# A gated linear recurrence with a solve in front: its lead-in in another order, products and zeroing on other engines

## The chip, the cores and the metric

The kernel runs on one core of a Trainium2 chip. Time is device time of one launch, in microseconds (us), as the median of three runs. Engines: PE is TensorE, DVE is VectorE, ACT is ScalarE, POOL is GpSimd, SP is SyncE, which issues most DMAs. A "q" behind an engine (SPq) is its queue.

## The reference, cut to what matters

```python
# attention part: B, H, S, D = 4, 8, 768, 40
for t in range(S):
    y[:, :, t] = np.einsum('bhd,bhde->bhe', rt, state)
    Sa = np.einsum('bhde,bhe->bhd', state, at)
    state_decay = state * wt[:, :, None, :] - np.einsum('bhd,bhe->bhde', Sa, bt)
    state = state_decay + np.einsum('bhd,bhe->bhde', vt, kt)
# then, on the 3072 rows of y: a mixture of 8 experts (top 2 by noisy logits),
# then w_in, h * tanh(softplus(h)), w_out
```

## The kernel before, in words

The 32 heads' sequences of 768 steps are cut into 24 chunks of C = 32 steps. A chunk is taken in two halves of 16 heads, so the state passes through NG = 48 turns of the recurrence; turn g belongs to chunk g // 2. Inside a chunk the steps are made independent by a triangular system, and chunks are solved four at a time (GJ = 4): solve 0 serves chunks 0 to 3 (turns 0 to 7), solve 1 chunks 4 to 7, and so on.

**Per chunk i.** `load_w` and `load` fetch w and a (tile wa), and k and b (tile kb). `scale` (L218) runs a decay scan E (L225), a reciprocal (L228), a backward scan R (L229) and the product abd (L234) on VectorE, then scales kb by R (L237, GpSimd); ScalarE makes copies (WE). `decays` (L244) copies E for the transposes. `prods` (L264) multiplies kb and abd on TensorE (L277) into a buffer of PSUM ring pp (two buffers); ScalarE copies it out twice (L282), to Ls, which goes to a DRAM scratch lscr, and to AM; `mask` (L285, GpSimd) masks the AM part. `turns` (L289) transposes kb and Ec on TensorE (L295) through ring pp; ScalarE copies the results to kn, which goes to DRAM and comes back into tile KB, and to EN. `scale_a` (L256) multiplies EN with AT (L261, a pair of GpSimd products) and asks for the AT load of chunk i + 2.

**Per four chunks.** `load_l` (L385) brings lscr back as tile Lu. `solve_group` (L388) inverts the triangular blocks in VectorE steps (L414, L416, then pairs of product L426 and reduction L429); solves 1 and on give two products to GpSimd. The result goes to DRAM (tscr, L463) and comes back in blocks (`tbd`, L357). `apply` (L364) multiplies blocks and AM on TensorE (L378) to tile Z.

**A turn of the recurrence** (`chain`, L586): s_mm (L541) and its VectorE eviction (L546, "s"), two groups of transposes `tr` (L558), u_mm of the next turn (L528), evicted by ScalarE (L531, "u eviction"), y_mm (L503), and rv_mm (L573) with its VectorE eviction (L584, "rv").

**The order** is written out by hand for TensorE, VectorE, ScalarE and GpSimd: what is emitted first runs first on its engine; SyncE issues in order of emission too. `begin` (L627) emits the lead-in of chunks 0 to 3. Then three generators (prepare, solve, apply) yield positions, and `pump` (L676) always advances the one with the lowest, up to the current one; a generator in `wants` can force another to go first. Positions of the lead-in are early(x) = -1 + x/42 (L315); turn c of the first eight stands at -.35 + 1.35 c/8 (`tau`, L622). Everything up to -.35 is emitted ahead of turn 0. Within a turn `pump` is called at (3, 6, 7, 8, 9, 9)/9 of it, the last two around rv_mm. Solve 0 advances x by the cost that its steps name:

```python
for t in range(1, h):                 # h = 8
    yield at(.38 + .0083 * t * t)
...
                yield at(.6)          # eight times
...
        yield at(.1 if i in pool else 1.2)   # pool is empty in solve 0
...
        yield at(1.2)                 # reductions, the last is add(5)
```

The OPT entry x places scale 4 at 4.6, the steps of chunk 4 at 5.2, of chunk 5 at 6.5, of chunk 6 at 12.5 and 21.5, of chunk 7 at 28; apply 0 stands at z0 = 20.9, and solve 1 at s_1, from -.45 to .6; because its load stands at -.51 and wants the products of chunks 4 to 7, these and scale 8 are emitted right behind solve 0.

Of the kernel before, what the change touches and what calls it, by code (L numbers as in the profile page):

```python
# [21 lines left out]
C = 32  # L22
# [5 lines left out]
OPT = dict(yd=(), yv=33, gix=(1, 3, 4), ye=(2, 2),  lag2=1, x=(4.6, 5.2, 6.5, 12.5, 21.5, 28, 28, 28), dl=0, dk=0, ns=(0, 0), nw=(1, 1), va=1, rb=0, ra=1, kb=0, ry=(2, 2), p1=(0, 0, 0, 1, 1, 1), lw=((4, 2, 2), (6, 6, 6)), fl=((0, 1, 2, 2, 2, 2, 2, 2), (0,) * 8), lag=6, ll=.06, hurry=40, pool=(1, 4), rvpool=False, f=(3, 3, 1, 1, 1, 0), s=(.05, .72), s_1=(-.45, .6), tl=1.9, zl=.96, zd=.32, t0=-.35, nd=3, z0=20.9)  # L28
# [37 lines left out]
class Rec:  # L66


    def __init__(self, ctx, nc, tc, ins, emit_x, ident, share, late):
# [15 lines left out]
        self.Y = {}  # L85
# [3 lines left out]
    def consts_a(self):  # L89
# [22 lines left out]
        self.d1b = []  # L112
        for i in range(2):
            t = one.tile([128, 2 * PR * (C + 1) + 1], F32, name=f"d1b{i}")
            nc.vector.memset(t, 0.0)
            self.d1b.append(t)
            self.abd.append(one.tile([128, PR, 2, C], F32, name=f"abd{i}"))
# [33 lines left out]
    def consts_d(self):  # L151
        nc = self.nc
        nc.gpsimd.memset(self.Tt, 0.0)
        nc.gpsimd.memset(self.Tt[:, 0:C * C:C + 1], 1.0)
        nc.gpsimd.memset(self.Z[2][96:128], 0.0)
        self.gaps(0, GJ + 2)
# [5 lines left out]
    def fill_kb(self, i):  # L162
        nc, t = self.nc, self.KB[i]
        for c in range(2):
            if i:
                nc.scalar.copy(out=t[0:64, c], in_=self.zero[0:64, None, None, 0:D].to_broadcast([64, 2, HH, D]))
                yield
# [3 lines left out]
    def consts_c(self):  # L171
# [9 lines left out]
        yield  # L181
        self.ST, self.KB, self.RR, self.R2, self.rbd = [], [], [], [], []
        for i in range(3):
            t = one.tile([128, PR, 2, 64], F32, name=f"ST{i}")
            nc.vector.memset(t, 0.0)
            self.ST.append(t)
        for i in range(2):
            t = one.tile([128, 2, HH, C], F32, name=f"RR{i}")
            nc.vector.memset(t[0:64], 0.0)
            self.RR += [t[:, 0], t[:, 1]]  # L190
            self.R2.append(t)
        for i in range(2):
            self.rbd.append(one.tile([128, 2, PR, 2, C], F32, name=f"rbd{i}"))
            nc.gpsimd.memset(self.rbd[i], 0.0)
            self.KB.append(self.kbs[i].rearrange("p (x c h d) -> p c x h d", x=2, c=2, h=HH))
            if i == 0:
                nc.vector.memset(self.kbs[i][0:64], 0.0)

# [19 lines left out]
    def scale(self, i):  # L218
# [8 lines left out]
        d1b = self.d1b[i % 2]  # L227
# [7 lines left out]
        if GJ <= i + 2 < len(self.seq):  # L235
            self.load_w(i + 2)
        nc.gpsimd.tensor_tensor(out=m(kb), in0=m(kb), in1=Rv.to_broadcast([RW, 2 * PR, 2, C]), op=ALU.mult)  # L237
# [26 lines left out]
    def prods(self, i):  # L264
# [16 lines left out]
        for out, k in ((ls, 1), (am[:, :, 64:96], 0)):  # L281
            nc.scalar.mul(out=out, in_=pt.rearrange("p (q s x) -> p q s x", s=2, x=C)[:, :, k], mul=-1.0)  # L282
        (nc.scalar if i < OPT['dl'] else nc.sync).dma_start(out=self.lscr[i // GJ][i % GJ * PR:i % GJ * PR + PR].rearrange("u q t i -> (q t) u i"), in_=ls)

    def mask(self, i):  # L285
        m = self.AM[i % (2 * GJ)][:, :, 64:96]
        self.nc.gpsimd.tensor_tensor(out=m, in0=m, in1=self.mml[:, None, :].to_broadcast([128, PR, C]), op=ALU.mult)

    def turns(self, i):  # L289

        nc = self.nc
        pt4 = lambda: self.pp.tile([128, 512], F32, name="pp")
# [25 lines left out]

    def prepare(self):
        n = len(self.seq)  # L320
        x = OPT["x"]
        start = ((x[1],) * 6, (x[2],) * 6, (x[3],) * 2 + (x[4],) * 4, (x[5], x[6]) + (x[7],) * 4)
        for i in range(GJ, n):
            pos = iter([i / GJ - 2 + s / (6 * GJ) if i >= 2 * GJ else self.early(start[i - GJ][s]) for s in range(6)])
            if i == GJ:
                yield self.early(x[0])
                for _ in self.scale(i):
                    pass
                self.decays(GJ - 1)
                for _ in self.turns(GJ - 1):  # L330
                    pass
                self.scale_a(GJ - 1)
                self.gaps(6, 2)
                self.decays(i)
            sc = iter(())
            yield next(pos)
            if i + 1 < n:
                sc = self.scale(i + 1)
                next(sc)
            yield next(pos)  # L340
            next(sc, None)
            if i + 1 < n:
                self.decays(i + 1)
            self.prods(i)
            self.mask(i)
            if i + 2 < n:
                self.load(i + 2)
            for _ in self.turns(i):
                yield next(pos)
            self.scale_a(i)  # L350

# [33 lines left out]
    def load_l(self, k):  # L385
        self.nc.sync.dma_start(out=self.Lu[:, 0:C * C], in_=self.lscr[k].rearrange("u q t i -> (u q) (t i)"))
# [240 lines left out]
    def begin(self):  # L627

        for i in range(GJ):
            for _ in self.scale(i):  # L630
                pass
            if i < 2:
                self.decays(i)
            if i:
                self.prods(i - 1)
        self.prods(GJ - 1)
        self.load_l(0)
        self.consts_d()
        for x in self.consts_c():
            pass  # L640
        self.setup()
        for i in range(2):
            self.load_at(i)
        for i in range(GJ):
            self.mask(i)
        for i in range(GJ - 1):
            if i > 1:
                self.decays(i)
# [1058 lines left out]
```

## Time and profile before

| what | value |
|---|---|
| median of 3 runs | 1312.58 us (1310.92 to 1316.44) |
| the profiled execution | 1308.13 us, span of its trace 1306.3 us |
| busy shares of the span | PE 88%, DVE 67%, ACT 54%, POOL 45% |
| mean granted TensorE clock | 0.939 |
| first solve starts on VectorE | 36.86 us |
| first u eviction (turn 0) | 99.15 us |
| seventh u eviction (turn 6) | 149.43 us |
| last u eviction (turn 47) | 487.14 us |

The shares are means over stages with different limits. The lead-in and the first turns, about 150 us, are where the change is made, so the windows and timelines of that stretch are read.

### The profile page before, as it was taken

Reading aid. Unit: us, or ns where it says so; the run is one execution under the profiler, and the core shown is the slowest. Engines: PE = TensorE matmul, PEld = TensorE weight load, DVE = VectorE, ACT = ScalarE, POOL = GpSimd, SP = SyncE. Lnnn points to the kernel's source line nnn. Section 1 sums busy time; section 2 is a strip of 40 time slices with the busy share of each in tenths; the row PEclk is TensorE's granted clock in tenths of the full one; section 3 lists DMA queues with packets and bytes.
Section 4 is the critical chain, followed back from the end, with each engine's and each line's share of the span. In section 5 each row is a group of like instructions: output and inputs, shape, how many; then the busy total and the mean of one; then the engine's idle time right before and its main releaser. Section 6 shows DMA issues by size and latency. Waiting matters only on the chain. (4 is left out here: it accounts for less than half of the span.)

```text
span 1306.3 us, 34038 instructions
## 1 busy us (share of the span) xinstructions
PE 1154.5 (88%) x13902; PEld 1106.0 (85%) x13902; DVE 873.7 (67%) x1593; ACT 703.4 (54%) x1477; POOL 593.8 (45%) x535
## 2 busy tenths in 40 slices
PE   3538888889789787998999999899989999999998
PEld 3427778778678787998989999888989999999998
DVE  8778879696949345548679787585475556655543
ACT  4516676666556464334334344242476666666664
POOL 5744636363636142524335443352455455553331
PEclk9559989999889799999999999889999999999999
DMA  6755676768356575563464565563361111110000
GB/s 173 207 132 134 171 187 178 189 155 208 85 118 113 107 134 117 121 192 117 127 178 143 149 192 154 179 179 111 93 186 46 36 31 31 31 36 16 11 12 21
DMA packets 144941, 156.83 MB, mean 120 GB/s; under 512 B 70906, under 2 KB 113914, under 8 KB 144762
## 3 DMA queue, kind: packets, MB, share of 16 engines
q1 hardware_dynamic: 127546, 120.52, 35.9%
q0 software_dynamic: 10752, 22.32, 6.4%
q10 hardware_dynamic: 6464, 11.54, 3.1%
q8 instruction: 120, 1.97, 0.7%
q14 instruction: 59, 0.48, 0.1%
HBM read 111.20 MB, written 43.12 MB: 118 GB/s over the span
## 5 line engine op out<-in xcount | busy, mean ns | idle before, releaser
L1579 POOL TENSOR_TENSOR gl<-fh,gh 128x1024 fp32r<-128x1024 f32 x46 | 131.1, 2879 | 105.2 <-ACT gh L1595 101.8
L1234 PE MATMUL ph<-xh,w1h 128*128 128x256 f32 (+1 forms) x576 | 161.5, 293 | 9.7 <-issue 4.8
L1234 PE MATMUL ph<-xl,w1h 128*128 128x256 f32 (+1 forms) x576 | 161.1, 292 | 0.0
L1547 PE MATMUL fps<-fxh,ih 128*128 128x256 f32 x576 | 156.3, 286 | 1.3 <-DVE fh L1549 1.3
L1547 PE MATMUL fps<-fxl,ih 128*128 128x256 f32 x576 | 153.7, 281 | 0.5 <-DVE fxl L1090 0.3
L1578 DVE TENSOR_TENSOR fh<-fh,fp 128x1024 f32<-128x1024 f32 x48 | 95.0, 2014 | 60.3 <-ACT fp L1577 60.3
L1253 PE MATMUL py<-w2h,hh 128*128 128x320 f32 x400 | 129.8, 324 | 1.2 <-ACT y L1259 0.8
L1253 PE MATMUL py<-w2l,hh 128*128 128x320 f32 x400 | 126.0, 315 | 2.4 <-DVE w2l L1090 2.3
L1088 DVE SCALAR_TENSOR_TENSOR hl<-ph,hh 128x512 fp32r<-128x512 f32 (+1 forms) x104 | 69.3, 666 | 86.9 <-ACT hh L1086 86.5
L1253 PE MATMUL py<-w2h,hl 128*128 128x320 f32 x400 | 126.1, 315 | 1.2 <-DVE hl L1088 1.1
L1234 PEld LDWEIGHTS ph<-xh,w1h 128*128 128x128 f32 x576 | 113.1, 196 | 10.6 <-issue 10.4
L1549 DVE COPY fh<-fps 128x512 f32<-128x512 f32 x96 | 64.8, 689 | 78.8 <-ACT fp L1548 73.7
L1609 PE MATMUL fpy<-oh,gl 128*128 128x320 f32 x384 | 114.6, 310 | 0.0
L1609 PE MATMUL fpy<-oh,gh 128*128 128x320 f32 x384 | 114.3, 310 | 0.0
L1609 PE MATMUL fpy<-ol,gh 128*128 128x320 f32 x384 | 113.9, 308 | 0.0
L1234 PEld LDWEIGHTS ph<-xl,w1h 128*128 128x128 f32 x576 | 113.1, 196 | 0.4 <-DVE xl L1090 0.3
L1234 PE MATMUL ph<-xh,w1l 128*128 128x256 f32 (+1 forms) x384 | 112.1, 292 | 0.4 <-DVE w1l L1090 0.4
L1547 PEld LDWEIGHTS fps<-fxh,ih 128*128 128x128 f32 x576 | 109.0, 189 | 1.7 <-DVE fh L1549 1.6
L1547 PEld LDWEIGHTS fps<-fxl,ih 128*128 128x128 f32 x576 | 109.0, 189 | 1.1 <-DVE fxl L1090 1.1
L1086 ACT ACTIVATE hh<-ph 128x512 fp32r<-128x512 f32 (+1 forms) x104 | 59.9, 580 | 90.0 <-PE ph L1234 87.4
L1547 PE MATMUL fps<-fxh,il 128*128 128x256 f32 x384 | 107.8, 281 | 0.0
L261 POOL TENSOR_TENSOR share<-AT,EN 64x320 f32<-64x320 f32 x48 | 60.7, 1264 | 82.9 <-ACT EN L312 57.6
(271 smaller groups left out, 3278.0 us busy)
## 6 DMA issues: line engine op xcount, KB each, us to landing
share<-in_w_dram SPq DMA_DIRECT2D x9, 1280.0 KB
share<-in_w_dram SPq DMA_DIRECT2D x9, 1024.0 KB
wa<-in_wa_dram SPq DMA_DIRECT2D x40, 195.2 KB
knd<-kn SPq DMA_DIRECT2D x24, 320.0 KB
kb<-in_kb_dram SPq DMA_DIRECT2D x40, 192.0 KB
KB<-knd SPq DMA_DIRECT2D x24, 320.0 KB
yb<-y SPq DMA_DIRECT2D x22, 320.0 KB
ST<-in_vn_dram SPq DMA_DIRECT2D x48, 128.0 KB
```

The costliest lines, as they stand in the source:

```text
L261: self.nc.gpsimd.tensor_tensor(out=self.AM[i % (2 * GJ)][64 * ab:64 * ab + 64, :, 0:D], in0=self.AT[r, ab], in1=en[r, ab], op=ALU.mult)
L1086: nc.scalar.activation(out=hi, in_=src, func=AF.Relu if relu else AF.Copy)
L1088: nc.vector.scalar_tensor_tensor(out=lo, in0=src, scalar=0.0, in1=hi.bitcast(F32), op0=ALU.max, op1=ALU.subtract)
L1234: nc.tensor.matmul(ph[:, m % c], lhsT=a, rhs=b, start=(q == 0), stop=(q == len(ops) - 1))
L1253: nc.tensor.matmul(py, lhsT=a[:, m, ts], rhs=b[:, m], start=(m == 0 and q == 0), stop=(m == FC - 1 and q == 2))
L1547: nc.tensor.matmul(ph[:, i], lhsT=a, rhs=b, start=(q == 0), stop=(q == len(ops) - 1))
L1549: nc.vector.tensor_copy(h[:, 2 * m2:2 * m2 + 2], ph)
L1578: mul = lambda s: nc.vector.tensor_tensor(out=h[:, s], in0=h[:, s], in1=p[:, s], op=ALU.mult)
L1579: low = lambda s: (nc.vector if last and s.start % 8 else nc.gpsimd).tensor_tensor(out=gl[:, s], in0=h[:, s], in1=gh[:, s].bitcast(F32), o ...
L1609: nc.tensor.matmul(py, lhsT=a[:, m, ts], rhs=w[:, m], start=(q == 0), stop=(q == len(ops) - 1))
```

## The change

Chunks 0 to 3: the transposes of chunk i - 1 are emitted right behind its products, inside the loop over the scales, and use PSUM ring cs (four buffers) instead of pp. The kb products of chunks 0 to 7 move from GpSimd to VectorE; the masks of chunks 0 to 3 too, where one VectorE instruction reads the product from PSUM in place of a ScalarE copy and a GpSimd product. Scale 4 is emitted in `begin`, ahead of the first solve. A plan, a list of (1 for scale and decays or 0 for products, mask and turns, chunk, position), replaces x; solve 1 now runs from -.12 to .62 and apply 0 stands at 22. The Lu load of solve 0 is cut in four, one per chunk. The w and kb loads are asked for earlier. Memsets: ST and one d1b (of two) stay on VectorE, at the very start; RR goes to GpSimd, KB 0 to ScalarE; Tt, Z, rbd, mrv and the AM gaps stay on GpSimd and go ahead of the chunks.

```diff
@@ -25,7 +25,7 @@
 NG = NP * NC
-OPT = dict(
...
-x=(4.6, 5.2, 6.5, 12.5, 21.5, 28, 28, 28),
...
-s_1=(-.45, .6),
...
-z0=20.9)
+OPT = dict(
...
+plan=((0, 4, -0.881), (1, 5, -0.499), (1, 6, -0.498), (0, 5, -0.495), (1, 7, -0.493), (0, 6, -0.316), (0, 7, -0.249), (1, 8, -0.020)),
...
+s_1=(-.12, .62),
...
+z0=22)
@@ -82,7 +82,7 @@
         self.KN, self.ZT, self.EN, self.WE = {}, {}, {}, {}
-        self.Y = {}
+        self.Y, self.pls = {}, {}
@@ -109,11 +109,14 @@
         nc.gpsimd.memset(self.d1[:, :, 0:1], -1.0)
-        self.d1b = []
+        self.d1b = one.tile([128, 2 * PR * (C + 1) + 1], F32, name="d1b")
+        nc.vector.memset(self.d1b, 0.0)
+        self.ST, self.KB, self.RR, self.R2, self.rbd = [], [], [], [], []
+        for i in range(3):
+            t = one.tile([128, PR, 2, 64], F32, name=f"ST{i}")
+            nc.vector.memset(t, 0.0)
+            self.ST.append(t)
         for i in range(2):
-            t = one.tile([128, 2 * PR * (C + 1) + 1], F32, name=f"d1b{i}")
-            nc.vector.memset(t, 0.0)
-            self.d1b.append(t)
@@ -153,7 +156,7 @@
         nc.gpsimd.memset(self.Z[2][96:128], 0.0)
-        self.gaps(0, GJ + 2)
+        self.gaps(0, 6)
@@ -162,9 +165,8 @@
         for c in range(2):
-            if i:
-                nc.scalar.copy(out=t[0:64, c], in_=self.zero[0:64, None, None, 0:D].to_broadcast([64, 2, HH, D]))
-                yield
+            nc.scalar.copy(out=t[0:64, c], in_=self.zero[0:64, None, None, 0:D].to_broadcast([64, 2, HH, D]))
+            yield
@@ -178,24 +180,14 @@
                                     fill=1.0, base=0, channel_multiplier=1)
-        yield
-        self.ST, self.KB, self.RR, self.R2, self.rbd = [], [], [], [], []
-        for i in range(3):
-            t = one.tile([128, PR, 2, 64], F32, name=f"ST{i}")
-            nc.vector.memset(t, 0.0)
-            self.ST.append(t)
-        for i in range(2):
-            t = one.tile([128, 2, HH, C], F32, name=f"RR{i}")
-            nc.vector.memset(t[0:64], 0.0)
-            self.RR += [t[:, 0], t[:, 1]]
-            self.R2.append(t)
         for i in range(2):
             self.rbd.append(one.tile([128, 2, PR, 2, C], F32, name=f"rbd{i}"))
             nc.gpsimd.memset(self.rbd[i], 0.0)
+            t = one.tile([128, 2, HH, C], F32, name=f"RR{i}")
+            nc.gpsimd.memset(t[0:64], 0.0)
+            self.RR += [t[:, 0], t[:, 1]]
+            self.R2.append(t)
             self.KB.append(self.kbs[i].rearrange("p (x c h d) -> p c x h d", x=2, c=2, h=HH))
-            if i == 0:
-                nc.vector.memset(self.kbs[i][0:64], 0.0)
-
@@ -224,7 +216,7 @@
                                      initial=0.0, op0=ALU.mult, op1=ALU.add)
-        d1b = self.d1b[i % 2]
+        d1b = self.d1b
@@ -232,9 +224,10 @@
         nc.vector.tensor_tensor(out=abd[0:RW], in0=a[0:RW], in1=E[0:RW, :, :, 0:C], op=ALU.mult)
-        if GJ <= i + 2 < len(self.seq):
-            self.load_w(i + 2)
-        nc.gpsimd.tensor_tensor(out=m(kb), in0=m(kb), in1=Rv.to_broadcast([RW, 2 * PR, 2, C]), op=ALU.mult)
+        nxt = i + 4 if i < 2 else i + 2
+        if max(GJ, i + 2) <= nxt < len(self.seq) and i not in (2, 3):
+            self.load_w(nxt)
+        (nc.vector if i < 2 * GJ else nc.gpsimd).tensor_tensor(out=m(kb), in0=m(kb), in1=Rv.to_broadcast([RW, 2 * PR, 2, C]), op=ALU.mult)
@@ -278,18 +271,24 @@
         ls = self.p2.tile([128, PR, C], F32, name="Ls")
-        for out, k in ((ls, 1), (am[:, :, 64:96], 0)):
-            nc.scalar.mul(out=out, in_=pt.rearrange("p (q s x) -> p q s x", s=2, x=C)[:, :, k], mul=-1.0)
+        pv = pt.rearrange("p (q s x) -> p q s x", s=2, x=C)
+        self.pls[i] = pv[:, :, 0]
+        for out, k in ((ls, 1), (am[:, :, 64:96], 0))[:1 if i < GJ else 2]:
+            nc.scalar.mul(out=out, in_=pv[:, :, k], mul=-1.0)
         (nc.scalar if i < OPT['dl'] else nc.sync).dma_start(out=self.lscr[i // GJ][i % GJ * PR:i % GJ * PR + PR].rearrange("u q t i -> (q t) u i"), in_=ls)
 
     def mask(self, i):
-        m = self.AM[i % (2 * GJ)][:, :, 64:96]
-        self.nc.gpsimd.tensor_tensor(out=m, in0=m, in1=self.mml[:, None, :].to_broadcast([128, PR, C]), op=ALU.mult)
+        m, b = self.AM[i % (2 * GJ)][:, :, 64:96], self.mml[:, None, :].to_broadcast([128, PR, C])
+        pv = self.pls.pop(i)
+        if i < GJ:
+            self.nc.vector.scalar_tensor_tensor(out=m, in0=pv, scalar=-1.0, in1=b, op0=ALU.mult, op1=ALU.mult)
+            return
+        self.nc.gpsimd.tensor_tensor(out=m, in0=m, in1=b, op=ALU.mult)
 
...
         nc = self.nc
-        pt4 = lambda: self.pp.tile([128, 512], F32, name="pp")
+        pt4 = lambda: self.cs.tile([128, 512], F32, name="cs") if i < GJ else self.pp.tile([128, 512], F32, name="pp")
@@ -316,39 +315,39 @@
         return -1 + x / 42
+    def decayed(self, i):
+
+        yield from self.scale(i)
+        self.decays(i)
+
+    def turned(self, i):
+
+        self.prods(i)
+        self.mask(i)
+        yield from self.turns(i)
+        if i + 3 < len(self.seq):
+            self.load(i + 3)
+        self.scale_a(i)
+
     def prepare(self):
         n = len(self.seq)
-        x = OPT["x"]
-        start = ((x[1],) * 6, (x[2],) * 6, (x[3],) * 2 + (x[4],) * 4, (x[5], x[6]) + (x[7],) * 4)
-        for i in range(GJ, n):
-            pos = iter([i / GJ - 2 + s / (6 * GJ) if i >= 2 * GJ else self.early(start[i - GJ][s]) for s in range(6)])
-            if i == GJ:
-                yield self.early(x[0])
-                for _ in self.scale(i):
-                    pass
-                self.decays(GJ - 1)
-                for _ in self.turns(GJ - 1):
-                    pass
-                self.scale_a(GJ - 1)
-                self.gaps(6, 2)
-                self.decays(i)
-            sc = iter(())
+        for first, i, at in OPT["plan"]:
+            yield at
+            for _ in (self.decayed if first else self.turned)(i):
+                yield at
+        for i in range(2 * GJ, n):
+            pos = iter([i / GJ - 2 + s / (6 * GJ) for s in range(6)])
+            nxt = self.decayed(i + 1) if i + 1 < n else iter(())
             yield next(pos)
-            if i + 1 < n:
-                sc = self.scale(i + 1)
-                next(sc)
+            next(nxt, None)
             yield next(pos)
-            next(sc, None)
-            if i + 1 < n:
-                self.decays(i + 1)
-            self.prods(i)
-            self.mask(i)
-            if i + 2 < n:
-                self.load(i + 2)
-            for _ in self.turns(i):
+            for _ in nxt:
+                pass
+            turned = self.turned(i)
+            next(turned)
+            for _ in range(4):
                 yield next(pos)
-            self.scale_a(i)
-
+                next(turned, None)
@@ -383,7 +382,10 @@
     def load_l(self, k):
-        self.nc.sync.dma_start(out=self.Lu[:, 0:C * C], in_=self.lscr[k].rearrange("u q t i -> (u q) (t i)"))
+        for j in range(0, GJ, 1 if k == 0 else GJ):
+            m = 1 if k == 0 else GJ
+            self.nc.sync.dma_start(out=self.Lu[32 * j:32 * j + 32 * m, 0:C * C],
+                                   in_=self.lscr[k][j * PR:(j + m) * PR].rearrange("u q t i -> (u q) (t i)"))
@@ -626,44 +628,43 @@
     def begin(self):
-        for i in range(GJ):
-            for _ in self.scale(i):
-                pass
-            if i < 2:
-                self.decays(i)
-            if i:
-                self.prods(i - 1)
-        self.prods(GJ - 1)
-        self.load_l(0)
+        full = lambda it: [None for _ in it]
         self.consts_d()
-        for x in self.consts_c():
-            pass
-        self.setup()
+        self.consts_c()
         for i in range(2):
             self.load_at(i)
         for i in range(GJ):
-            self.mask(i)
-        for i in range(GJ - 1):
+            full(self.scale(i))
             if i > 1:
-                self.decays(i)
-            for _ in self.turns(i):
-                pass
+                self.mask(i - 2)
+            self.decays(i)
+            if i:
+                self.prods(i - 1)
+            if i in (1, 2):
+                full(self.turns(i - 1))
+                self.load((6, 4)[i - 1])
+        self.mask(GJ - 2)
+        self.prods(GJ - 1)
+        self.load_l(0)
+        for i in range(2, GJ):
+            full(self.turns(i))
+            if i == 2:
+                self.load(5)
+        full(self.fill_kb(0))
+        full(self.scale(GJ))
+        self.mask(GJ - 1)
+        self.setup()
+        for i in range(GJ):
             self.scale_a(i)
-            if i == 0:
-                self.load_v(0)
-                self.load_r(0)
-                self.load_rbd(0)
-            elif i == 1:
-                self.load(GJ)
-                for _ in self.fill_kb(0):
-                    pass
-                self.load_kb(0)
-            else:
-                self.load(GJ + 1)
-                self.load_v(1)
-                for _ in self.fill_kb(1):
-                    pass
-                self.load_kb(1)
+        self.gaps(6, 2)
+        self.decays(GJ)
+        self.load_kb(0)
+        self.load_v(0)
+        self.load_r(0)
+        self.load_rbd(0)
+        self.load_v(1)
+        full(self.fill_kb(1))
+        self.load_kb(1)
```

## Rows read from the trace of the kernel before

**Rows 1.** The chain that ended last, its earliest piece: start us, us, what.

```profile
911.23 0.97 issue
```

**Rows 2.** Windows: us, busy us of PE, PEld, DVE, ACT, POOL, clock, DMA, GB/s.

```profile
36.86:86.80 49.94, 22.06 (x328) 17.80 (x328) 46.57 (x51) 18.31 (x44) 33.54 (x24) 0.51 0.64 160
...
90.20:100.28 10.08, 5.73 (x61) 5.05 (x63) 0.01 (x1) 1.99 (x4) 2.73 (x2) 0.56 0.82 191
...
100.28:149.40 49.12, 41.35 (x948) 36.90 (x943) 47.32 (x66) 32.25 (x88) 27.65 (x16) 0.93 0.54 140
...
149.40:168.00 18.60, 16.78 (x376) 15.01 (x374) 10.34 (x15) 13.18 (x39) 6.86 (x5) 1.00 0.82 191
```

**Rows 3.** Timeline of the lead-in: start us, us, engine, line, operation [idle before <-releaser].

```profile
5.29 1.26 DVE L225 TENSOR_TENSOR_SCAN E<-wa,d 104x528 f32<-104x528 f32 x1 [3.29 <-DMA wa<-in_wa_dram]
...
8.28 2.47 POOL L237 TENSOR_TENSOR kb<-kb,R 104x1024 f32<-104x1024 f32 x1 [5.11 <-DVE R L229]
...
8.63 3.23 DVE L225 TENSOR_TENSOR_SCAN E<-wa,d 104x528 f32<-104x528 f32 x1
...
24.31 2.54 POOL L237 TENSOR_TENSOR share<-share,R 104x1024 f32<-104x1024 f32 x1 [2.85 <-DVE R L229]
...
31.72 0.35 SPq L386 DMA_DIRECT2D Lu<-lscr  x1
...
36.86 0.20 DVE L414 TENSOR_TENSOR tm<-Tt,Lu 128x4 f32<-128x4 f32 x1 [4.01 <-DMA Lu<-lscr]
```

**Rows 4.** Timeline, three single operations of VectorE and GpSimd.

```profile
54.97 1.05 DVE L426 TENSOR_TENSOR tm<-Tt,P 128x512 f32<-128x512 f32 x1
...
55.23 0.42 POOL L132 MEMSET share<- 128x384 f32 x1
...
112.71 1.20 DVE L426 TENSOR_TENSOR tm<-Tt,Lu 128x1024 f32<-128x1024 f32 x1
```

**Rows 5.** Groups by form, 0 to 150 us: count | busy us, mean ns | idle before.

```profile
L584 DVE TENSOR_TENSOR RR<-cs,mrv 64x256 f32<-64x256 f32 x10 | 4.2, 423 | 0.6 <-PE cs L573 0.5
...
L194 POOL MEMSET rbd<- 128x1024 f32 x2 | 1.8, 951 | 0.1
...
L426 DVE TENSOR_TENSOR tm<-Tt,P 128x512 f32<-128x512 f32 x4 | 4.1, 1036 | 0.0
...
L546 DVE TENSOR_TENSOR ST<-cs,WE 40x320 f32<-40x320 f32 x12 | 5.8, 487 | 0.2
```

**Rows 6.** Timeline of SyncE and GpSimd ahead of the second solve.

```profile
96.07 0.34 SPq L386 DMA_DIRECT2D Lu<-lscr  x1
...
103.42 1.99 POOL L261 TENSOR_TENSOR share<-AT,EN 64x320 f32<-64x320 f32 x2 [10.49 <-issue]
...
105.44 0.47 SPq L254 DMA_DIRECT2D AT<-in_at_dram  x1
```

**Rows 7.** Timeline: last reductions of the first solve, first two u evictions.

```profile
84.48 2.33 DVE L429 TENSOR_REDUCE Tt<-tm 128x64 f32<-128x1024 f32 x2
...
99.15 0.86 ACT L531 COPY ST<-cs 32x320 f32<-32x320 f32 x2 [1.36 <-PE cs L528]
...
105.11 0.86 ACT L531 COPY ST<-cs 32x320 f32<-32x320 f32 x2
```

**Rows 8.** Windows of VectorE's scales 4 to 7 within the first solve.

```profile
44.97:48.30 3.33, 0.59 (x4) 0.59 (x5) 3.26 (x5) 1.71 (x5) 0.00 (x0) 0.50 0.82 214
...
48.90:54.37 5.47, 2.60 (x69) 2.06 (x68) 5.40 (x5) 2.35 (x7) 5.04 (x3) 0.50 1.05 239
...
56.02:62.73 6.71, 5.23 (x82) 4.17 (x81) 4.24 (x6) 3.24 (x10) 6.16 (x4) 0.50 0.88 268
...
71.14:74.54 3.40, 0.42 (x3) 0.42 (x4) 3.26 (x6) 1.93 (x6) 0.28 (x1) 0.50 0.16 48
```

**Rows 9.** Timeline of TensorE: half of turns 7, products 8.

```profile
100.80 0.93 PE L295 MATMUL pp<-ident,kb 104*128 104x104 f32 x8
...
128.67 1.10 PE L277 MATMUL pp<-kb,abd 40*32 40x64 f32 x64
```

More of the change, by code (lines that the diff above doesn't have):

```diff
@@ L27 @@
 NG = NP * NC
-OPT = dict(yd=(), yv=33, gix=(1, 3, 4), ye=(2, 2),  lag2=1, x=(4.6, 5.2, 6.5, 12.5, 21.5, 28, 28, 28), dl=0, dk=0, ns=(0, 0), nw=(1, 1), va=1, rb=0, ra=1, kb=0, ry=(2, 2), p1=(0, 0, 0, 1, 1, 1), lw=((4, 2, 2), (6, 6, 6)), fl=((0, 1, 2, 2, 2, 2, 2, 2), (0,) * 8), lag=6, ll=.06, hurry=40, pool=(1, 4), rvpool=False, f=(3, 3, 1, 1, 1, 0), s=(.05, .72), s_1=(-.45, .6), tl=1.9, zl=.96, zd=.32, t0=-.35, nd=3, z0=20.9)
+OPT = dict(yd=(), yv=33, gix=(1, 3, 4), ye=(2, 2),  lag2=1, plan=((0, 4, -0.881), (1, 5, -0.499), (1, 6, -0.498), (0, 5, -0.495), (1, 7, -0.493), (0, 6, -0.316), (0, 7, -0.249), (1, 8, -0.020)), dl=0, dk=0, ns=(0, 0), nw=(1, 1), va=1, rb=0, ra=1, kb=0, ry=(2, 2), p1=(0, 0, 0, 1, 1, 1), lw=((4, 2, 2), (6, 6, 6)), fl=((0, 1, 2, 2, 2, 2, 2, 2), (0,) * 8), lag=6, ll=.06, hurry=40, pool=(1, 4), rvpool=False, f=(3, 3, 1, 1, 1, 0), s=(.05, .72), s_1=(-.12, .62), tl=1.9, zl=.96, zd=.32, t0=-.35, nd=3, z0=22)
 NW = 2 * PR * (C + 1)
```

## The prediction

> **What bounds the kernel now.** I read the chain that ended last first, to learn what the lead-in has to do with the end. Followed back from the last instruction it goes only to 911 us [rows 1], far behind the recurrence. So a gain in the lead-in counts only as a shift: it must move the recurrence, whose order is fixed, and with it all that follows.
>
> Then I read busy time by stage. The reader should see two things [rows 2]. In the first solve (36.86 to 86.80) VectorE is busy 46.57 of 49.94 us, and the recurrence can't begin before that solve is stored: VectorE bounds the lead-in. Then VectorE stands idle for 10.08 us, while the solved blocks go out and back. From 100.28 to 149.40, turns 0 to 5 of the recurrence, it is busy 47.32 of 49.12 us: second solve, scales of chunks 9 to 11, evictions. So VectorE bounds these turns too; TensorE, at 41.35, has room. From 149.40 on VectorE has slack (10.34 of 18.60), TensorE little (16.78). What counts is therefore not when turn 0 starts, but when VectorE has done everything due by turn 6.
>
> **Where the order puts things.** Prepare and solve steps go out by position, -1 + x/42. The solve's first seven steps sum to x = 3.82, eight small ones to 8.62, then come twelve of 1.2: the last two reductions stand at 20.62 and 21.82. The plan's -0.499 to -0.493 are x = 21.04 to 21.29. So the scales of chunks 5 to 7 go out ahead of the last reduction, and the store of the solve stays behind them; the same arithmetic puts every scale of before where the trace has it. The turns of chunks 6 and 7 (-0.316, -0.249) fall into turn 0, scale 8 (-0.020) into turn 1, and the second solve starts at -0.12, turn 1.36; before, these chunks' products, scale 8 and the start of that solve went out ahead of turn 0.
>
> **Step 1, start of the first solve.** Undisturbed, scans, reciprocal and product of one chunk take 3.34 us (first scan 5.29 to second 8.63 [rows 3]). The kb product isn't in the trace on VectorE; the nearest row, a two-input product of 1024 columns, is 1.20 [rows 4], the high end GpSimd's own 2.47 [rows 3]. I take 1.20, the same engine and width: 4.54 a chunk, 18.2 for four, plus one mask from PSUM at 0.42 (nearest: the PSUM eviction of 256 columns [rows 5]): 23.9. Against this: the second scan took 3.23 us beside a GpSimd product of 2.47 where the first took 1.26 [rows 3], 0.8 us lost per us of product. The EN products of chunks 0 and 1 (a pair 1.99 [rows 6]) now run beside scans: 0 to 3.2 us, I take 2.5. So the last kb product ends at 26.4, not 26.85 (24.31 + 2.54 [rows 3]): almost no gain. The way to the Lu load (31.72) is 4.87 as before: 31.3. That load took 5.14 whole [rows 3] and 4.21 at the second solve (96.07 to 100.28 [rows 2, 6]); its last quarter takes from 1.1 (a quarter of 4.21) to 5.1, I take 3.0. Start at 34.3 instead of 36.86. Meanwhile VectorE does two masks, scale 4 and mask 3 (5.8 us): ready at 32.2, so they cost nothing; with a faster load they would be late next. Product 3 on TensorE also needs the PSUM buffer that mask 1 reads; mask 1 follows the last kb product, 0.4 that the masks above stand for. At nothing go: VectorE's memsets (they leave a wait for the Lu load), the transposes of chunks 0 and 1 on the cs ring (TensorE idles between products), ScalarE's two further zero copies and SyncE's earlier kb and wa loads (under the first solve). If the loads crowded out the Lu load, its upper end above is the price.
>
> **GpSimd's memsets beside the scans.** Seven of about 0.95 us each [rows 5] move to the front. Only one memset of before lies beside a two-input product: 0.42 us in a product of 1.05, where four such average 1.036 [rows 4, 5]. So I cost them at 0; the other end is 0.8 x 6.7 = 5.3. The Trainium skill (GPSIMD Engine Reference, Key points) says that GpSimd shares its SBUF interfaces with VectorE and contends with instructions that have two SBUF inputs, and it excepts no memset. By that rule the sum would be 5.3 us worse; the trace agrees with it for products, and for its one memset it does not.
>
> **Step 2, the first solve.** Of its 49.95 us (36.86 to 86.81 [rows 3, 7]) the four scales with their waits take 3.33, 5.47, 6.71 and 3.40 [rows 8], together 18.9; its own steps 31.0. Scale 4 now lies ahead, the 2.3 us wait for wa in the third stretch goes (loads come earlier), and the kb products of chunks 4 to 7 and the first masks leave GpSimd. Own steps: 31.0 at most; at least about 27, the second solve (47.32 less 10.1 of evictions [rows 2, 5] and three scales of 3.35). I take 29.3. Scales 5 to 7: 3 x (3.35 + 1.20) = 13.7, plus 1.6 for mask and EN products of chunk 5 beside them: 15.2. End at 34.3 + 29.3 + 15.2 = 78.8 instead of 86.81: 8.0 us gained (3 to 14).
>
> **Step 3, turn 0.** From the solve's end to the first u eviction is 12.34 us (86.81 to 99.15 [rows 7]), unchanged: 91.1. Turn 0 took 5.96 (99.15 to 105.11 [rows 7]). It now holds also products 6 and 7 (1.10 each) and the transposes of turns 6 (two lots of 0.93 and a short wait, 2.04 [rows 9]), with two evictions of 0.3 between: 4.9 more. The next u eviction is at 102.0: 3.1 ahead of before.
>
> **Step 4, the second solve starts late.** SyncE issues its Lu load behind the AT load of chunk 9, which waits for GpSimd's EN products of chunk 7 (before: they ran 103.42 to 105.41, AT issued 105.44 [rows 6]). EN 7 was ready 1.7 ahead of the u eviction (103.42 to 105.11 [rows 6, 7]); with one pair of transposes fewer between I take 1.3, so 100.7; plus 1.99; three issues of some 0.5: Lu issued at 104.2, landed at 108.4 (105 to 111). VectorE's order has rv 1 and s 2 behind its first step, so they wait too. Before, it began at 100.28.
>
> **Step 5, what VectorE still has to do.** The stretch of 49.12 us, less the 2.8 of evictions now done (rv 0, s 0, s 1 [rows 5]), plus scale 8 (3.4, hidden before in the idle stretch) and some 1.1 for its kb product on GpSimd: 50.8. End at 159.2 instead of 149.40: 9.8 late. TensorE's idle share after that (1.8 of 18.6) gives back perhaps 1.3.
>
> **Sum:** -8.0 up to the store, +17.8 from there to turn 6 (80.4 against 62.6), -1.3: +8.5 us. The profiled execution, 1308.13 us with 1.8 around its span, would be 1316.6; it lies 4.5 below the median of the runs shown, and on that median (1312.58) I forecast 1321.1.
>
> **Rivals.** (a) *The chain, not VectorE, sets turns 1 to 5.* For: TensorE is busy 84% there too [rows 2]. Then turn 1's lead of 3.1 us stays: 1309.5; with no EN products in the way of the scans (-2.5), own steps of 27 (-2.3) and a Lu quarter in 1.1 instead of 3.0 (-1.9), 1302.8, faster. It decides if VectorE is busy under some 85% between its second solve's start and turn 6. Against: 96% now, with less idle time ahead of it to come. (b) *VectorE bounds, but the terms fall short:* Lu at 105 instead of 108.4 and 2.5 off the lead-in: +2.6, 1315, no difference to be told. (c) *GpSimd's memsets hold up the first scans:* +5.3, 1326; the rule named above, for which this trace has one row against it. (d) *The scales do stand behind the whole solve:* then it ends at 63.6, turn 0's evictions wait for the scales until 79, the second solve starts near 94 and turn 6 some 4.5 earlier: 1308. Against: the positions.
>
> **How the numbers follow.** About 0.5%, 6.6 us, is what a measurement can tell from no change: under 1306.0 is faster, over 1319.1 slower. The forecast has 0.43, (c) 0.06: slower 0.49. (b) has 0.15, the nearer end of (a) and (d) 0.12: within 0.5%, 0.27. The far end of (a) has 0.24: faster; more than its rows bear out, because the sum rests on a difference of two large terms. The likeliest case alone reaches from 1315 to 1329 (each end from Lu, own steps and the start). The range goes down to (a)'s far end and leaves out (c)'s tail: 1302 to 1329.
>
> **What would show it.** First Lu-fed step at 34 us (31 to 37); scans of chunks 1 to 3 mostly at 1.26; kb products on VectorE at 1.2; three scales ahead of the solve's last reduction, its store near 79; first u eviction near 91, 11 us to the next; VectorE idle for over 20 us around them, then busy over 95% to turn 6, the seventh u eviction near 159. The forecast is wrong if turn 6 comes ahead of 149.4, or if VectorE idles behind the second Lu load.

## The result, and the profile after

The changed kernel is slower, by 15.2 us where 8.5 were forecast: 1328.74 us (1323.31 to 1331.95, median of 4 runs) beside 1313.59 (1310.92 to 1316.44, 4 runs), a ratio of 1.0111 with a 95% interval of 1.0068 to 1.0153. Forecast: 1321.1, from 1302 to 1329, slower; the time lies 0.3 us inside the upper end. The profiled execution took 1327.01 us with a span of 1325.2, 18.9 more than before.

| what | before | after |
|---|---|---|
| first solve step | 36.86 | 33.79 |
| last reduction of the first solve ends | 86.81 | 75.01 |
| first u eviction (turn 0) | 99.15 | 86.94 |
| second solve's first step | 100.28 | 104.24 |
| seventh u eviction (turn 6) | 149.43 | 155.36 |
| last u eviction (turn 47) | 487.14 | 508.03 |

So 11.8 us won at the store of the first solve are lost by turn 6 and 5.9 more with them; then 15.0 more go between turns 6 and 47, and from there to the end 2.0 come back.

VectorE's timeline of the lead-in, after (as [rows 3] and [rows 7]):

```profile
5.27 1.26 DVE L217 TENSOR_TENSOR_SCAN E<-wa,d 104x528 f32<-104x528 f32 x1 [0.61 <-DMA wa<-in_wa_dram]
...
8.61 1.23 DVE L230 TENSOR_TENSOR kb<-kb,R 104x1024 f32<-104x1024 f32 x1
9.77 1.26 DVE L217 TENSOR_TENSOR_SCAN E<-wa,d 104x528 f32<-104x528 f32 x1
...
18.21 1.88 DVE L230 TENSOR_TENSOR kb<-kb,R 104x1024 f32<-104x1024 f32 x1
...
20.35 1.77 DVE L217 TENSOR_TENSOR_SCAN E<-KB,d 104x528 f32<-104x528 f32 x1
...
24.40 1.21 DVE L230 TENSOR_TENSOR share<-share,R 104x1024 f32<-104x1024 f32 x1
...
33.79 0.17 DVE L416 TENSOR_TENSOR tm<-Tt,Lu 128x4 f32<-128x4 f32 x1 [2.71 <-DMA Lu<-lscr]
...
57.93 1.20 DVE L431 TENSOR_REDUCE Tt<-tm 128x64 f32<-128x1024 f32 x1
59.05 1.24 DVE L217 TENSOR_TENSOR_SCAN E<-wa,d 104x528 f32<-104x528 f32 x1
...
72.67 1.21 DVE L230 TENSOR_TENSOR kb<-kb,R 104x1024 f32<-104x1024 f32 x1
73.80 1.21 DVE L431 TENSOR_REDUCE Tt<-tm 128x128 f32<-128x1024 f32 x1
88.69 0.99 DVE L548 TENSOR_TENSOR ST<-cs,WE 40x320 f32<-40x320 f32 x2 [13.69 <-PE cs L543]
97.90 0.88 DVE L586 TENSOR_TENSOR RR<-cs,mrv 64x256 f32<-64x256 f32 x2 [8.22 <-PE cs L575]
...
104.24 0.17 DVE L416 TENSOR_TENSOR tm<-Tt,Lu 128x4 f32<-128x4 f32 x1 [4.09 <-DMA Lu<-lscr]
```

Read it from the top. The kb product on VectorE takes 1.2 us. Ahead of the first solve only steps of chunks 2 and 3 meet GpSimd's EN products and are slower (chunk 2's kb product 1.88, chunk 3's first scan 1.77). From 59.05 to 73.80 the scales of chunks 5 to 7 stand ahead of the last reduction. Behind it VectorE idles 13.69, 8.22 and 4.09 us. The windows say the same by stage: us, then busy us of PE, PEld, DVE, ACT, POOL, clock, DMA, GB/s (as [rows 2]).

```profile
33.79:74.95 41.16, 7.97 (x96) 6.18 (x95) 40.33 (x49) 15.56 (x32) 12.87 (x11) 0.56 0.58 149
74.95:104.24 29.29, 20.09 (x426) 17.34 (x427) 2.85 (x7) 13.54 (x36) 4.88 (x6) 0.81 0.60 153
104.24:156.12 51.88, 32.64 (x729) 29.34 (x726) 50.64 (x64) 25.55 (x70) 30.19 (x15) 0.82 0.45 107
```

VectorE works 2.85 of 29.29 us, then 50.64 of 51.88. Before, its idle stretch was 10.08 us and the busy one 49.12 [rows 2].

What it waits for between is seen on the other engines: timeline of ScalarE, GpSimd and SyncE, after (as [rows 6] and [rows 7]).

```profile
86.94 0.86 ACT L533 COPY ST<-cs 32x320 f32<-32x320 f32 x2 [0.85 <-PE cs L530]
...
90.55 0.73 POOL L286 TENSOR_TENSOR share<-share,mml 128x256 f32<-128x256 f32 x1 [18.36 <-ACT share L277]
...
96.62 1.77 POOL L254 TENSOR_TENSOR share<-AT,EN 64x320 f32<-64x320 f32 x2 [1.39 <-issue]
...
97.41 0.86 ACT L533 COPY ST<-cs 32x320 f32<-32x320 f32 x2
...
98.42 0.47 SPq L247 DMA_DIRECT2D AT<-in_at_dram  x1
...
99.62 0.37 SPq L387 DMA_DIRECT2D Lu<-lscr  x1
...
155.36 0.86 ACT L533 COPY ST<-cs 32x320 f32<-32x320 f32 x2 [0.54 <-PE cs L530]
```

Chunk 7's EN products end at 98.39; SyncE then issues AT (98.42) and, one load later, Lu (99.62). That is the way named under step 4.

### The profile page after: what moved, and what is told of

The parts are those of the page before. It is cut to its first block, busy times and chain, and to the rows that moved or that the text cites. A ratio compares the mean times of both kernels' runs of the same rounds, so it can differ in the third digit from the quotient of the medians.

```text
span 1325.2 us, 34053 instructions
## 1 busy us (share of the span) xinstructions
PE 1154.2 (87%) x13902; PEld 1108.1 (84%) x13902; DVE 872.9 (66%) x1601; ACT 704.7 (53%) x1475; POOL 573.7 (43%) x525
## 5 line engine op out<-in xcount | busy, mean ns | idle before, releaser
L1549 ACT ACTIVATE fp<-fps 128x512 f32<-128x512 f32 x96 | 56.0, 596 | 79.3 <-PE fps L1548 75.0
```

Source lines behind the costliest of these rows:

```text
L1549: nc.scalar.activation(out=p[:, 2 * m2:2 * m2 + 2], in_=ph, func=AF.Sigmoid, scale=-1.0)
```

## The experiments

The first four ran on a chip where the kernel before took 1332.42 us (25 runs), the next four where it took 1315.18 (18 runs), the last four where it took 1314.01 (23 runs). Each ratio is to the kernel before on its own chip. The u evictions are those of the one profiled execution of each kernel. Where turns are compared with the kernel before, on the second chip its profile is `before_again`.

| run | us | ratio, 95% interval | u eviction 0 | 6 | 27 | 47 |
|---|---|---|---|---|---|---|
| kb_loads_back | 1345.09 | 1.0112, 1.0038 to 1.0187 | 87.01 | 155.10 | 340.50 | 521.02 |
| kb_loads_late | 1337.03 | 1.0026, 0.9993 to 1.0058 | 99.15 | 149.45 | 337.16 | 515.22 |
| scales_behind | 1342.49 | 1.0066, 1.0036 to 1.0096 | 78.57 | 150.06 | 337.81 | 516.00 |
| turns_ahead | 1331.02 | 0.9992, 0.9965 to 1.0020 | 88.50 | 139.65 | 330.64 | 509.46 |
| before_again | one run, 1317.45 | | 99.68 | 149.86 | 336.26 | 494.88 |
| after_again | 1330.08 | 1.0103, 1.0074 to 1.0133 | 87.55 | 156.25 | 350.42 | 509.70 |
| kb_loads_back_again | 1326.88 | 1.0095, 1.0063 to 1.0126 | 87.05 | 155.74 | 342.40 | 499.31 |
| turns_ahead_kb | 1306.71 | 0.9934, 0.9910 to 0.9959 | 89.93 | 141.30 | 323.80 | 478.79 |
| scale8_late | 1310.84 | 0.9975, 0.9953 to 0.9997 | 88.53 | 145.77 | 333.18 | 491.02 |
| kb_products_back | 1309.56 | 0.9956, 0.9930 to 0.9983 | 94.07 | 145.95 | 331.65 | 484.08 |
| scales_behind_kb | 1303.67 | 0.9910, 0.9877 to 0.9943 | 85.40 | 137.93 | 326.14 | 482.50 |
| lu_whole | one run, 1308.64 | | 91.84 | 142.41 | 329.34 | 483.06 |

Up to turn 6 one execution can be set beside another: kernels that do the same up to there agree within 1.2 us at turn 6, whatever the chip (149.43, 149.45 and 149.86; 155.10 to 156.25). Later they can't be told apart to a few us: `before` and `before_again` are the same kernel and differ by 2.4 us at turn 27 and 7.7 at turn 47, where at most 1 us was expected up to turn 31.

### What is put into turn 0: `turns_ahead`, `turns_ahead_kb`

```diff
-(0, 6, -0.316), (0, 7, -0.249), (1, 8, -0.020)), ... s_1=(-.12, .62)
+(0, 6, -0.480), (0, 7, -0.479), (1, 8, -0.478)), ... s_1=(-.45, .6)
```

> The changed kernel with products and turns of chunks 6 and 7 and scale 8 ahead of apply 0 and the second solve from -.45 to .6, as before. Theory E (VectorE idles in turns 0 and 1 because the second solve's load waits for these turns): second solve's first step near 88 us instead of 104, turn 0 down from 10.5 to about 5, seventh u eviction near 140, the later loss of about 13 us stays; time 1312 to 1318 us. Rival F (the chain's own pace sets turns 1 to 6): only turn 0's 5 us come back, 1322 to 1325 us.

> Products and turns of chunks 6 and 7 and scale 8 ahead of apply 0, the second solve from -.45 to .6, and the kb loads where they were before. Theories A and E together: turn 6 near 140 as without the loads (9.8 us ahead of before), and at turn 27 still 8 to 10 us ahead instead of 3.2; ratio 0.992 to 0.996, faster than both kernels. Rival B or F: as turns_ahead alone, 0.999, or back at 1.00 because later waits take the lead away whatever the loads do.

`turns_ahead_kb` has this edit and that of `kb_loads_back` (below). With products and turns of chunks 6 and 7, scale 8 and the second solve put ahead together, the second solve starts at 90.67 (`turns_ahead`) and 91.88 (`turns_ahead_kb`) instead of 104.24; turn 0 takes 4.15 us instead of 10.47: theory E, and rival F falls. On one chip turn 6 comes 14.4 us earlier than in `kb_loads_back_again` (141.30 against 155.74), which has the same loads of later chunks, and the time falls from 1326.88 to 1306.71, under the kernel before. The windows of `turns_ahead_kb`:

```profile
76.24:91.88 15.64, 10.62 (x135) 8.92 (x127) 4.17 (x5) 5.40 (x13) 5.28 (x5) 0.57 0.80 209
91.88:141.30 49.42, 38.39 (x898) 34.48 (x897) 46.91 (x66) 30.79 (x85) 26.51 (x14) 0.93 0.56 137
```

The gap is 15.64 us, with scale 8 inside it, instead of 29.29; the bound stretch is as long as before the change. So the loss up to turn 6 is in where these steps stand; the rest of the change, without the moved loads of later chunks and taken together, gains (0.66% in `turns_ahead_kb`). `turns_ahead`, which has those loads still, can't be told from the kernel before (0.9992).

### Scale 8 alone: `scale8_late`

```diff
-(1, 8, -0.478)
+(1, 8, -0.020)
```

> turns_ahead_kb with scale 8 alone back at the changed kernel's position in turn 1; the turns of chunks 6 and 7 and the start of the second solve stay ahead. Theory A (from the second solve's first step to turn 6 VectorE sets the time, and what moves out of its idle stretch into that one is paid in full): first u eviction and the second solve's first step stay within 1 us of turns_ahead_kb's (9.8 and 8.8 ahead of the kernel before); scale 8 took VectorE 4.3 us there (76.16 to 80.48), so the seventh u eviction comes 3.5 to 5 us later, some 4 ahead of the kernel before instead of 8.6; ratio about 0.996. Theory B (only the second solve's start counts): the seventh u eviction stays within 1.5 us of 8.6 ahead; ratio about 0.993.

First u eviction at 88.53, second solve at 91.26, turn 6 at 145.77: 4.5 us later than in `turns_ahead_kb`, for a scale that took 4.3 there. The window from the second solve to turn 6:

```profile
91.26:145.77 54.51, 38.84 (x889) 34.87 (x889) 52.25 (x70) 31.45 (x87) 29.47 (x15) 0.86 0.50 126
```

It is 5.1 us longer, and VectorE is busy 5.3 us more in it. Theory A: in this stretch a step on VectorE is paid in full, and in the gap it is nearly free (the second solve starts 0.6 us sooner without it).

### The scales of chunks 5 to 7: `scales_behind`, `scales_behind_kb`

```diff
-(1, 5, -0.499), (1, 6, -0.498), (0, 5, -0.495), (1, 7, -0.493)
+(1, 5, -0.470), (1, 6, -0.469), (0, 5, -0.468), (1, 7, -0.467)
```

In `scales_behind_kb`, which starts from `turns_ahead_kb`, the next three entries follow at -0.466 to -0.464.

> The changed kernel with the scales of chunks 5 to 7 and the turns of chunk 5 behind the last reduction of the first solve and behind apply 0. Theory C (a store that waits behind three scales starts the chain and the second solve late): solve stored near 60 us instead of 75, first u eviction near 77 instead of 87, second solve's first step near 95 instead of 104, seventh u eviction near 146 instead of 155, time about 9 us under the changed kernel's, 1318 to 1321 us. Rival D (only VectorE's sum of work counts, wherever the scales stand): seventh u eviction within 2 us of 155, time as the changed kernel's.

> turns_ahead_kb with the scales of chunks 5 to 7 behind the first solve's last reduction. Theory A (what counts is when VectorE has done everything due by turn 6; the second solve's load waits for products 6 and 7 in either order): store 15 us earlier, near 60; the second solve's first step within 1.5 us of turns_ahead_kb's 91.9 and the seventh u eviction within 2 us of 8.6 ahead of the kernel before; ratio 0.991 to 0.996, no difference to be told from turns_ahead_kb's 0.9934. Theory B (the way of the solved blocks through DRAM, 12 us from the store to turn 0, is what holds the second solve up): first step 3 us or more earlier, seventh u eviction over 11.5 ahead, ratio 0.990 or less.

In `scales_behind` the store comes at 59.85 instead of 75.04, and turn 0 at 78.57; but the second solve starts at 99.00, only 5.2 us sooner than in the changed kernel's profile, and turn 6 at 150.06, 5.3 sooner: between theory C (146) and rival D (155). In `scales_behind_kb` theory A failed on the trace: the second solve starts at 87.39, 4.5 sooner than in `turns_ahead_kb`, and turn 6 3.4 sooner. The timeline of SyncE shows why. First `turns_ahead_kb`, then `scales_behind_kb`:

```profile
76.27 0.34 SPq L467 DMA_DIRECT2D tscr<-Tt  x1
...
80.24 1.81 SPq L362 DMA_DIRECT2D Tbd<-tscr  x4
...
83.11 0.47 SPq L247 DMA_DIRECT2D AT<-in_at_dram  x1
83.68 0.53 SPq L278 DMA_DIRECT2D lscr<-Ls  x1
...
87.26 0.33 SPq L389 DMA_DIRECT2D Lu<-lscr  x1
```

```profile
80.00 0.54 SPq L278 DMA_DIRECT2D lscr<-Ls  x1
80.59 1.57 SPq L362 DMA_DIRECT2D Tbd<-tscr  x3
83.36 0.34 SPq L389 DMA_DIRECT2D Lu<-lscr  x1
```

ScalarE had written chunk 7's Ls by 77.6 in the first and 78.3 in the second. In the first its store stands on SyncE behind the Tbd loads, which wait for the solve's store, and a kb and an AT load, and goes out at 83.68; in the second at 80.00. Lu follows about 3.5 us behind in both. So the way of the solved blocks through DRAM holds up the second solve, as in theory B, by the order on SyncE; the ratio, 0.9910, stands at the edge of theory A's range and doesn't reach theory B's. By turn 27 the lead over `turns_ahead_kb` is gone (326.14 against 323.80): the third solve's Lu took 7.7 us (159.43 to 167.16) against 6.6. The profile of `scales_behind_kb` is of its slowest execution (1309.54, median 1303.67), so this says little. The times, 0.9910 and 0.9934, have overlapping intervals, so which of the two is the better is not told; both beat both kernels.

### The kb loads of later chunks: `kb_loads_back`, `kb_loads_late`, `after_again`, `kb_loads_back_again`

In the changed kernel the kb load of chunk i + 3 goes out behind the turns of chunk i; before, that of chunk i + 2 went out between mask and turns. `kb_loads_back` puts it there again from chunk 8 on; `kb_loads_late` is the kernel before with these loads behind the turns.

```diff
         self.mask(i)
+        if i >= 2 * GJ and i + 2 < len(self.seq):
+            self.load(i + 2)
         yield from self.turns(i)
-        if i + 3 < len(self.seq):
+        if i < 2 * GJ - 1:
             self.load(i + 3)
```

> The changed kernel, but from chunk 8 on the kb load of chunk i + 2 is asked for between products and turns again, not that of chunk i + 3 behind the turns. Theory A (these loads now stand right ahead of the Lu load of the later solves, which then lands 7.5 us after its issue instead of 5.2 to 6.6): the lead-in and turns 0 to 6 stay as in the changed kernel (seventh u eviction near 155), the loss of 13 us between turn 10 and turn 47 goes, time 1314 to 1319 us. Rival B (all of the loss stems from VectorE's backlog in turns 1 to 6, the rest only passes it on): time as the changed kernel's, 1325 to 1330 us.

> The kernel before, with nothing but the kb loads from chunk 10 on moved behind the turns as in the change. Theory A: 10 to 14 us slower than before, 1323 to 1328 us, with the u evictions unchanged up to turn 7 and 2 to 4 us lost at each of the later solves. Rival B: within 3 us of before.

> The kernel before, unchanged, profiled beside the next three, since the first four experiments ran on a chip where the kernel before itself took 1332 us instead of 1313. Every theory expects a ratio of 1.00; up to turn 31 its u evictions should stand within 1 us of those shown, and what differs later (turns 33 to 45) belongs to the chip.

> The changed kernel, unchanged, on the same chip as the other three of this call. Every theory expects the ratio of before, 1.007 to 1.015; u evictions as in its first profile: seventh near 155, turn 10 some 2 us and turn 27 some 13 us behind the kernel before.

> The changed kernel with the kb loads of the recurrence where they were before. Theory A, now with its size from the u evictions (at turn 27 it stood 6.7 us behind the kernel before, the changed kernel 13.0): 5 to 7 us less than the changed kernel of this call, a ratio of 1.005 to 1.008. Rival B: the same ratio as the changed kernel, within 0.2%.

By the times theory A isn't borne out. On the first chip the ratio of `kb_loads_back`, 1.0112, is that of the changed kernel elsewhere, as rival B has it, and `kb_loads_late` lost 0.26% with 1 inside the interval, where theory A had 10 to 14 us. On the second, 1.0095 for `kb_loads_back_again` beside 1.0103 is rival B again. The traces show more. SyncE ahead of the third solve, after and then before:

```profile
173.99 1.76 SPq L195 DMA_DIRECT2D kb<-in_kb_dram  x2
175.86 0.48 SPq L247 DMA_DIRECT2D AT<-in_at_dram  x1
...
177.10 0.58 SPq L387 DMA_DIRECT2D Lu<-lscr  x1
```

```profile
170.24 0.48 SPq L254 DMA_DIRECT2D AT<-in_at_dram  x1
...
172.04 0.58 SPq L386 DMA_DIRECT2D Lu<-lscr  x1
...
175.49 2.00 SPq L203 DMA_DIRECT2D kb<-in_kb_dram  x2
```

After, the two halves of a kb load stand 3.1 us ahead of the Lu load, which feeds VectorE's first step at 184.93, 7.8 us after its issue; before, the kb load went 3.5 us behind it and Lu took 5.2 (172.04 to 177.19). Over the third to fifth solves it is 7.1 to 7.8 after, 5.2 to 6.6 before; on the second chip 7.3 to 8.0 in `after_again`, 6.1 to 7.1 in `before_again`, 4.9 to 7.4 in `kb_loads_back_again`. (At the sixth VectorE comes later than the load in all of them.) The waits of VectorE from 160 to 500 us (us in all, times, longest), for before, after and `kb_loads_back_again`:

```profile
DVE tm L414 <- DMA Lu<-lscr: 13.4, 3, 5.6
```

```profile
DVE tm L416 <- DMA Lu<-lscr: 20.6, 3, 7.7
```

```profile
DVE tm L418 <- DMA Lu<-lscr: 14.4, 3, 6.0
```

On the second chip these are 15.2 (`before_again`), 21.2 (`after_again`) and 14.4: in the changed kernel 6 to 7 us of waits go with the loads. But three kernels on the first chip have the loads in that same place and don't have the waits, `scales_behind` (14.2 us) and, shown here, `kb_loads_late` and `turns_ahead`:

```profile
DVE tm L416 <- DMA Lu<-lscr: 14.1, 3, 5.9
```

```profile
DVE tm L416 <- DMA Lu<-lscr: 15.5, 3, 6.0
```

`kb_loads_back`, on that chip without them, waits 13.8. So the place of the loads alone doesn't make the wait; what else it takes, or whether the chip counts, stays open. On the second chip `kb_loads_back_again` stands level with `after_again` at turn 6 (155.74, 156.25), is 8.0 ahead at turn 27 and 10.4 at turn 47. Yet its span is only 3.9 shorter and its median 3.2, with overlapping intervals. From turn 47 to the end `after_again` took 819.3 us and it 825.8; the six other profiled executions of this chip and the third lie between 820.8 and 825.3, so 6.5 us of what was won by then was not kept, with the same instructions behind it. Whether that tail belongs to the kernel or to the execution stays open, and with it the size of this cause in time. `turns_ahead` and `turns_ahead_kb` differ by this edit alone, and their ratios, 0.9992 and 0.9934, have intervals apart; but they ran on two chips.

### The kb products: `kb_products_back`

```diff
-(nc.vector if i < 2 * GJ else nc.gpsimd).tensor_tensor(out=m(kb), ...
+nc.gpsimd.tensor_tensor(out=m(kb), ...
```

> turns_ahead_kb with the kb products of chunks 0 to 7 on GpSimd again, as before. Theory A (the prediction's: a GpSimd product costs VectorE 0.8 us for each of its own, so that moving the product to VectorE at 1.2 gains some 0.8 a chunk): first solve step 34.5 to 37 us instead of 33.8; the three scales of chunks 5 to 7 with scans of 2 to 3.3 us in place of 1.26 and no shorter than the 15.3 of now; store of the solve at 75 to 78; ratio 0.994 to 0.998. Theory B (the product is merely added work for VectorE): eight products of 1.2 gone, first solve step 1 to 3 us earlier than 33.8, store at 68 to 71, ratio about 0.989.

The first solve starts at 35.22 instead of 33.81, its store goes out at 80.17 instead of 76.27, turn 6 is 4.65 us later. Theory A, with the store 2 us beyond its range; theory B falls. The timeline of VectorE and GpSimd:

```profile
37.92 0.68 DVE L418 TENSOR_TENSOR tm<-Tt,Lu 128x100 f32<-128x100 f32 x1
...
65.90 2.48 POOL L230 TENSOR_TENSOR kb<-kb,R 104x1024 f32<-104x1024 f32 x1 [14.28 <-issue]
66.26 3.23 DVE L217 TENSOR_TENSOR_SCAN E<-wa,d 104x528 f32<-104x528 f32 x1
...
71.23 2.55 POOL L230 TENSOR_TENSOR kb<-kb,R 104x1024 f32<-104x1024 f32 x1 [2.85 <-ACT share L277]
71.65 3.24 DVE L217 TENSOR_TENSOR_SCAN E<-wa,d 104x528 f32<-104x528 f32 x1
```

A scan beside the product takes 3.23 instead of 1.25. So the three scales are hardly cheaper for VectorE without their products: 14.82 us (62.86 to 77.68) against 15.29 in `turns_ahead_kb` (59.74 to 75.03). The rest of the loss is that GpSimd comes late: its EN products now run beside the solve's small steps (0.68 where the same step took 0.26), so these and the next take 27.64 us up to the first scale, against 25.93. And the store, ready at 78.89, goes out at 80.17: it stands on SyncE behind an AT load, which waits for EN products until 78.47, and wa loads.

### The load in four: `lu_whole`

```diff
-for j in range(0, GJ, 1 if k == 0 else GJ):
-    m = 1 if k == 0 else GJ
+for j in range(0, GJ, GJ):
+    m = GJ
```

> turns_ahead_kb with the Lu load of the first solve in one piece. The prediction took 3.0 us from the issue of the last quarter, against 5.1 whole; the changed kernel took 4.90 from the first of the four issues, which themselves last 2.24. Theory A (the load waits for the last store of products and its cost is mostly its own latency, so cutting it in four gains nothing): first solve step within 0.5 us of 33.8. Theory B (the quarters overlap): first step 1.5 us or more later, 35.3 to 36. The time within 3 us of turns_ahead_kb's in either case.

```profile
30.60 0.38 SPq L389 DMA_DIRECT2D Lu<-lscr  x1
...
35.06 0.17 DVE L418 TENSOR_TENSOR tm<-Tt,Lu 128x4 f32<-128x4 f32 x1 [4.29 <-DMA Lu<-lscr]
```

First step at 35.06, 1.25 us later: between the two theories. From the first issue the quarters take no less (28.60 to 33.81, 5.2 us, against 4.46 whole), but the first goes out 2.0 us earlier.

## Why the prediction was right, and where its sizes were off

**Where the order puts things** held: the scales of chunks 5 to 7 ahead of the last reduction, products and turns of chunks 6 and 7 in turn 0, scale 8 behind the second solve's first steps.

**Step 1.** Start at 33.79, forecast 34.3. The kb product costs 1.21 to 1.23 undisturbed, where 1.20 was taken; the last one ends at 25.61 (forecast 26.4). The last quarter of the load, costed at 3.0, was issued at 30.83 and used 2.96 later.

**GpSimd's memsets** cost nothing, as taken: scans of 1.26 at 5.27 and 9.77, both beside memsets of 0.94 to 1.06 us. Rival (c) falls. GpSimd's own timeline shows who does pay:

```profile
5.47 1.06 POOL L135 MEMSET share<- 128x1152 f32 x1
...
6.66 3.26 POOL L181 TENSOR_SCALAR_AFFINE_SELECT mrv<-mrv 32x32 f32<-32x32 f32 x4
9.98 0.95 POOL L185 MEMSET rbd<- 128x1024 f32 x1
```

The select reads SBUF and takes 3.26 beside VectorE's scans and products, against 0.96 for four alike at 2.19, beside VectorE's memsets. The Trainium skill (SBUF — State Buffer, Who interferes with whom) has VectorE's instructions with two SBUF inputs contend with GpSimd instructions that read SBUF, not with those that only write it; this trace agrees with both halves.

**Step 2.** 25.26 us to the scales and a reduction of 1.21 are 26.5 for own steps, under the lower bound of 27 (29.3 taken): GpSimd is busy 12.87 us beside this solve instead of 33.54 [rows 2]. Three scales 14.75 (15.2 taken). Gain up to here 11.8, forecast 8.0.

**Step 3.** First to second u eviction 10.47 (86.94 to 97.41), forecast 10.9.

**Step 4.** Lu issued at 99.62 and used at 104.24; forecast 104.2 and 108.4. From the solve's end that is 29.2 us, forecast 29.6: step 2's gain carried over, and the way was as described.

**Step 5.** VectorE is busy from 104.24 to 156.12, 51.9 us, forecast 50.8. From the solve's end to turn 6 it is 80.35 us (75.01 to 155.36), against 62.62 before: +17.7, forecast +17.8.

**The term that failed** is the last: -1.3 after turn 6. Measured: 5.9 at turn 6, 18.9 in the span, so +13.0; on the second chip 6.4 and 13.3, so +6.9. Both lean on single executions (from turn 6 to the end `before` took 1156.9 us and `before_again` 1165.8); by the medians, 15.2 and 14.9 us slower, it is some 9. It goes back in part to a sentence of step 1, that SyncE's earlier kb and wa loads go at nothing, which looked at the first solve only, and to the view that the lead-in counts only as a shift of a recurrence whose order is fixed. The edit moves the kb loads of later chunks ahead of later Lu loads. In the changed kernel undoing this takes 6 to 7 us of VectorE's waits away; other kernels with the loads there have no such waits, no difference in time is clear, and the rest of the late loss wasn't traced. So why this term failed stays open. That the time still lies in the range, by 0.3 us, is partly luck: the lead-in came 3.8 us better than forecast and hid that much of it.

**The rivals.** (a) falls: VectorE is busy 98% from the second solve's start to turn 6. (b) came true in part: the lead-in was 3.8 us better than forecast, and Lu's 104 is that same gain, not a second one beside it as in (b)'s sum. So turn 6 stood at +5.9, where the forecast had +9.8 and (b) +3.9; the later loss hid it. (d) falls by the positions; `scales_behind`, which has its order, starts the second solve at 99.0 where (d) had 94, and loses 0.66% on its chip (interval 0.36 to 0.96).

## What to carry to other kernels

A solve that ends earlier is worth nothing if the engine that bounds the next stage then stands idle for a load: follow, on the engine that issues the DMAs in order, what the next solve's load stands behind, and put work of the bounding engine into its gap. Here a two-input product beside VectorE's scans cost it about as much on GpSimd as on VectorE itself (14.82 against 15.29 us for three scales), and GpSimd's lateness came on top. When a helper is rewritten for the lead-in, look at what its order does to every later chunk.

## What the runs showed of the hardware

On the chip of the first four runs, and in no trace of another chip here, TensorE lost time late in the recurrence in every kernel: turn 44 took 25.15 to 25.20 us in the four, 5.7 in `turns_ahead_kb` on another chip. In `turns_ahead` it stops between single matmuls with nothing to wait for ("issue"), while GpSimd issues indirect DMAs of 0.96 us each. TensorE's timeline, then GpSimd's:

```profile
475.65 0.31 PE L543 MATMUL cs<-ST,KB 128*40 128x40 f32 x6 [0.43 <-issue]
476.40 0.37 PE L543 MATMUL cs<-ST,KB 128*40 128x40 f32 x4 [0.44 <-issue]
477.86 0.26 PE L543 MATMUL cs<-ST,KB 128*40 128x40 f32 x1 [1.08 <-issue]
```

```profile
476.03 0.96 POOL L981 DMA_INDIRECT ids<-tok,POS  x1 [0.21 <-issue]
```

Why that chip alone does so wasn't tried, nor whether the indirect DMAs are the cause. It weighs on the four kernels alike, and the kernel before, which wasn't profiled there, took 1332.42 us; so the ratios of that chip are taken to hold, but its late turns are not set beside those of others.
